# A windowed-attention, soft-MoE and ReLU-squared kernel: attention on pairs of units, scores on four quarters of the array

## The chip, the cores and the metric

The kernel runs on one NeuronCore of a Trainium2 chip. The engines are TensorE (PE, with its weight loads shown apart as PEld), VectorE (DVE), ScalarE (ACT), GpSimd (POOL) and SyncE (SP), which here only issues DMAs. The metric is the device time of one execution in microseconds; the median of the runs counts.

## The reference

Three stages follow one another. Batch is 4, there are 8 heads, 576 positions, 64 dimensions a head. The first four heads see a plain window of 32 positions, the last four a window of 32 positions four apart (dilated).

```python
scores = scale * np.matmul(q, k.transpose(0, 1, 3, 2))          # scale = 1/8
scores = np.where(masks[None], scores, -1e9)
attn = np.exp(scores - np.max(scores, axis=-1, keepdims=True))
attn = attn / (np.sum(attn, axis=-1, keepdims=True) + 1e-9)
x = np.matmul(attn, v)                       # then (4*576, 512): 2304 tokens

logits = x @ phi                             # 32 slots, 4 for each of 8 experts
d = exp(logits - logits.max(0)); d /= d.sum(0) + 1e-9       # over all tokens
slot_input = (d.T @ x).reshape(8, 4, 512)
slot_out[e] = np.maximum(slot_input[e] @ w1[e], 0.0) @ w2[e]    # 1024 inner
c = exp(logits - logits.max(1)); c /= c.sum(1) + 1e-9       # over the slots
x = c @ slot_out

r = np.maximum(x @ w_in, 0.0)                # 2048 inner
out = (r * r) @ w_out
```

w_in and w_out arrive as 64-bit floats and are converted on the chip; all else is 32-bit.

## The kernel before, in words

**Units and chunks.** A unit is one batch and one pair of heads (`kc`): 16 units in all, with keys and queries laid out as 128 rows, 64 for each of its two heads. The dilated heads are stored so that their window is contiguous too. A unit has 9 blocks of 64 queries; each block needs 96 keys. Three blocks make a chunk, so there are 48 chunks of [128 query rows (2 heads x 64), 3 blocks, 96 keys], 12 a batch.

**A chunk's way.** Each step has one letter in the written order.

- `f0`, `f1`: `fill_qz` (L310 on DVE, L312 on ACT) copies the queries of each head, times -1/8, into a block-diagonal tile `qz`; the zeros beside them were written once at the start (L262).
- `q`: `ch_qk` writes the mask into a PSUM bank with an identity matmul (L320, bf16), and adds the scores of three blocks with three matmuls of 128 rows, 128 columns of weights and 96 columns that move (L323). The block-diagonal tile keeps the two heads apart.
- `m`: the minimum of the negated scores (L337, DVE). `x`: three exps with their sums (L343, ACT).
- `n`: the sum plus 1e-9 (L350) and its reciprocal (L351) on DVE, then the normalization on POOL (L352).
- `t`: three transposes (L358). `T`: the copy `pts` from PSUM (L363, DVE or ACT). `p`: six matmuls with the values, one for each block and head (L372). `P`: the copy of the result `o` into `x` transposed (L391, one piece for plain heads; L398, two pieces with a stride for dilated heads).
- `d`: `dup_v` on POOL (L199) repeats values that two neighbouring blocks share.

**A batch's way.** `L`: the logits (L443). `Le`, `L2`, `D`, `De`, `ce`, `cn`: the softmaxes over tokens and slots, with running maxima from batch to batch. `X`: transposes of x back (L409), `Xe` their copy (L420). `S`: sums of x into slots (L428), collected in one bank for all four `kc`, and `Se` the update of the running sums (L538, L540). The last batch has a version of its own, with slot sums one `kc` at a time (`Z`, L525), and the transposed slots (`st`, L566), from which the experts start.

**Order.** All engines follow an order written out by hand: the strings `PRE`, `ATT` (repeated for three batches) and `TAILSEQ` list the steps, and a token is skipped where its condition doesn't hold yet. Each engine works through its instructions in this order. Behind attention `SEQ` orders the experts (`y`, L759; `x`, L882), the conversion of w_in and w_out (L829 to L867) and the last stage (L979 to L1013), which takes the longest.

**Memory.** Loads go through one SP queue into a ring of 22 buffers: keys and queries, then values of every unit, then 16 loads of w1, 16 of w2 (1 MB each), then w_in and w_out, for which only five of the buffers serve. A load is issued when a buffer comes free, in this order: a unit's keys and queries are freed with the scores of its last chunk, its values with the last matmul on them. PSUM has eight banks: two each for scores, transposes and values, one for logits and x transposed back (`m`), one for slot sums.

```python
nc.tensor.matmul(s, lhsT=identb, rhs=mb[:, o:o + 3, :], start=True, stop=False)        # L320
for i in range(3):
    blk = 3 * c + i
    nc.tensor.matmul(s[:, i, :], lhsT=qz[n % QZ_BUFS][:, i, :],                        # L323
                     rhs=qk_t[u][1][:, QB * blk:QB * blk + KB], start=False, stop=(i == 2))
```

## Time and profile before

| | |
|---|---|
| median of 3 runs | 400.65 us (400.21 to 400.71) |
| profiled execution | 399.67 us |
| its span, first to last instruction | 397.9 us |
| mean granted clock of TensorE | 0.991 |
| busy share of the span | PE 97%, DVE 69%, ACT 62%, POOL 21% |
| moved by DMA | 70.11 MB |

The profile is of one execution. Busy time of an engine is the time in which it had an instruction under way; PE's matmuls are pipelined, so that PE counted as busy is not PE at its peak. One fp32 matmul shows as two records where the weights are loaded twice. The chain of waits goes back from the last instruction to what released it, step by step. A DMA share is the mean busy share of the core's 16 DMA engines, and can pass 1 a little.

### The profile page before, as it was taken

The page shows a single profiled execution, that of the slowest core. Times are in us where ns is not written, and L with a number is a line of the kernel's source. Part 1 is how long each engine was busy: PE and PEld are TensorE (multiplying, and loading weights), DVE is VectorE, ACT ScalarE, POOL GpSimd, SP SyncE. Part 2 cuts the span into 40 slices and gives each one's busy share as a digit, 9 for nine tenths or more (in the row PEclk, how much of TensorE's full clock was granted, in tenths as well). Part 3 has the DMA queues.
Part 4 walks back from the last instruction along what each step waited for, and adds up shares of the span by engine and source line. Part 5 has one row for each costly group of instructions (what it writes and reads, how often), then busy time and mean ns, then how long its engine had stood idle before and what let it go on. Part 6 is the DMA issues. An engine that isn't in the chain of part 4 may idle for free.

```text
span 397.9 us, 8017 instructions
## 1 busy us (share of the span) xinstructions
PE 387.8 (97%) x2880; PEld 296.3 (74%) x2880; DVE 274.1 (69%) x630; ACT 247.9 (62%) x738; POOL 83.8 (21%) x167
## 2 busy tenths in 40 slices
PE   7999999999999999899999999999999999999996
PEld 4887887887875334678776877788888888888885
DVE  3799888888763226999999999655454555544554
ACT  5688888888954104899698876564444445644450
POOL 2787775757621001110000002000000000000000
PEclk9699999999999999999999999999999999999999
DMA  7998599989989999963356200021000000400004
GB/s 220 417 417 328 182 296 298 325 306 294 316 313 343 390 387 377 387 210 117 111 208 211 107 0 2 0 105 55 0 2 0 0 2 1 158 2 1 0 2 158
DMA packets 31991, 70.11 MB, mean 176 GB/s; under 512 B 2256, under 2 KB 5328, under 8 KB 31952
## 3 DMA queue, kind: packets, MB, share of 16 engines
q1 hardware_dynamic: 31952, 69.61, 49.7%
q8 instruction: 23, 0.38, 0.4%
q14 instruction: 16, 0.13, 0.1%
HBM read 64.88 MB, written 4.72 MB: 175 GB/s over the span
## 4 chain that ended last, share of the span: by engine, by line
PE 66%; DVE 21%; issue 4%; DMA 4%; SPq 2%; ACT 1%; POOL 0%; DVEq 0%; POOLq 0%; ACTq 0%
PE acc L1007 23%; PE acc L1013 12%; PE s L323 6%; PE o L372 5%; DVE cv L847 4%; PE psh L759 4%; PE pt L358 4%; DVE lo L1001 3%; DVE slotA L842 3%; PE ph L979 3%; PE xnp L409 3%; DMA slotA<-in_w_in_dram 2%; PE s L320 2%; PE pacc L428 2%; DVE cv L838 2%
## 5 line engine op out<-in xcount | busy, mean ns | idle before, releaser
L1007 PE MATMUL acc<-wohl,hi 128*128 128x512 f32 x580 | 152.5, 396 | 0.0
L1007 PEld LDWEIGHTS acc<-wohl,hi 128*128 128x128 f32 x580 | 107.1, 189 | 22.7 <-issue 0.8
L986 ACT ACTIVATE u<-ph 128x384 f32<-128x384 f32 x96 | 46.4, 491 | 70.9 <-PE ph L979 69.8
L1013 PE MATMUL acc<-wohl,lo 128*128 128x512 f32 x290 | 84.9, 395 | 0.3 <-DVE lo L1001 0.2
L996 DVE TENSOR_TENSOR g<-u 128x384 f32<-128x384 f32 x74 | 41.1, 557 | 55.3 <-ACT u L986 55.3
L1013 PEld LDWEIGHTS acc<-wohl,lo 128*128 128x128 f32 x290 | 54.1, 188 | 13.8 <-DVE lo L1001 1.3
L1001 DVE TENSOR_TENSOR lo<-g,hi 128x384 fp32r<-128x384 f32 x96 | 52.8, 555 | 7.9
L343 ACT ACTIVATE p<-s,ns 128x96 f32<-128x96 f32 x144 | 47.4, 343 | 7.3 <-DVE ns L337 6.8
L994 ACT ACTIVATE hi<-u 128x384 fp32r<-128x384 f32 x82 | 42.9, 526 | 2.2
L352 POOL TENSOR_TENSOR p<-p,ns 128x288 f32<-128x288 f32 x48 | 32.1, 671 | 26.9 <-DVE ns L351 13.7
L713 POOL COPY c3n<-c_all 96x96 f32<-96x96 f32 x24 | 9.0, 412 | 108.9 <-PE ph L725 84.8
L343 ACT ACTIVATION_READ_ACCUMULATOR p<-s,ns 128x1 f32 x144 | 29.7, 206 | 0.0
L337 DVE TENSOR_REDUCE ns<-s 128x3 f32<-128x288 f32 x48 | 21.7, 451 | 10.7 <-PE s L323 10.4
L358 PE MATMUL pt<-ident,p 128*96 128x128 f32 x144 | 24.9, 284 | 0.6 <-POOL p L352 0.6
L199 POOL TENSOR_TENSOR slotC<-slotC,zero 32x384 f32<-32x384 f32 (+1 forms) x27 | 19.9, 746 | 6.6 <-DMA slotC<-in_vw_dram 5.5
L323 PEld LDWEIGHTS s<-slotC,qz 128*128 128x128 f32 x126 | 18.4, 216 | 2.1 <-issue 1.9
L323 PE MATMUL s<-slotC,qz 128*128 128x96 f32 x126 | 19.1, 293 | 0.7 <-DVE qz L310 0.7
L847 DVE CUSTOM_DVE_ANT_0 cv<-slotA,cv 128x2048 uint16<-128x2048 uint16 (+1 forms) x18 | 18.8, 1044 | 0.1
L842 DVE SCALAR_TENSOR_TENSOR slotA<-slotA 128x1024 int32<-128x1024 int32 (+1 forms) x18 | 18.7, 1041 | 0.2
L358 PEld LDWEIGHTS pt<-ident,p 128*96 128x96 f32 x144 | 16.6, 136 | 2.4 <-issue 1.1
L979 PE MATMUL ph<-C3a,M 96*128 96x384 f32 x48 | 16.3, 350 | 2.0 <-DVE M L957 1.1
L835 ACT ACTIVATE slotA<-slotA 128x1024 int32<-128x1024 uint32 (+1 forms) x18 | 18.0, 1004 | 0.2 <-DMA slotA<-in_w_in_dram 0.2
(182 smaller groups left out, 559.2 us busy)
## 6 DMA issues: line engine op xcount, KB each, us to landing
slotB<-in_w_dram SPq DMA_DIRECT2D x14, 1024.0 KB, 6.6
slotC<-in_w_dram SPq DMA_DIRECT2D x12, 1024.0 KB, 7.0
slotA<-in_w_in_dram SPq DMA_DIRECT2D x6, 1024.0 KB, 5.4
slotA<-in_w_out_dram SPq DMA_DIRECT2D x6, 1024.0 KB, 5.0
slotA<-in_w_dram SPq DMA_DIRECT2D x5, 1024.0 KB, 6.8
slotC<-in_kq_dram SPq DMA_DIRECT2D x6, 576.0 KB, 7.8
slotB<-in_kq_dram SPq DMA_DIRECT2D x6, 576.0 KB, 8.2
out_dram<-e SPq DMA_DIRECT2D x12, 256.0 KB, 2.2
```

What stands on the lines that cost most here:

```text
L323: nc.tensor.matmul(s[:, i, :], lhsT=qz[n % QZ_BUFS][:, i, :], rhs=qk_t[u][1][:, QB * blk:QB * blk + KB], start=False, stop=(i == 2),)
L343: nc.scalar.activation(p[:, i, :], s[:, i, :], AF.Exp, bias=ng[:, i:i + 1], scale=-1.0, accum_out=sm[:, i:i + 1])
L352: nc.gpsimd.tensor_tensor(p, p, rs.unsqueeze(2).to_broadcast([128, 3, KB]), op=ALU.mult)
L358: nc.tensor.transpose(pt[:, i, :], p[:, i, :], ident)
L842: nc.vector.scalar_tensor_tensor(w[:, :, 1], w[:, :, 1], -2 ** 31, w[:, :, 0], op0=ALU.bitwise_and, op1=ALU.bitwise_or)
L847: E[e].tensor_tensor(box["yi"], box["yi"], box["w"][:, :, 1], op=ALU.add)
L986: nc.scalar.activation(r, u_t[k], AF.Relu)
L994: nc.scalar.activation(t, r, AF.Square)
L996: nc.vector.tensor_tensor(t, r, r, op=ALU.mult)
L1001: nc.vector.tensor_tensor(lo, g_t.pop(k), hi_t[k], op=ALU.subtract)
L1007: nc.tensor.matmul(a[:, c], lhsT=hi_t[k][:, sl], rhs=w[:, c], start=first, stop=False)
L1013: nc.tensor.matmul(a[:, c], lhsT=lo_t[k][:, sl], rhs=wo_hl[fc][0][:, c], start=False, stop=last)
```

## The change

Attention is planned anew. A unit is now worked on together with its neighbour (the order of `kc` becomes 0, 1, 2, 3, so that both units of a pair have the same kind of window).

- `q` works for a pair: the array is addressed as four parts of 64 rows by 64 columns. The row half is the head, the column half is the unit. Each part gets the mask by a quarter of the identity and then three score matmuls, directly from the loaded queries; the results of the two row halves go to two PSUM banks. There are 24 pair steps with 4 mask matmuls and 12 score matmuls each. The queries' block-diagonal copies (`f0`, `f1`, `qz`) are gone.
- A group is one of the two banks: one head, two units, again [128, 3, 96]; 48 groups. Mask and scores are no longer negated or scaled, so `m` takes a maximum, negates it, and multiplies it by 1/8 in an instruction of its own (DVE, 128x3), and the exp scales by 1/8.
- `n` is split: `r` is the sum plus 1e-9 and the reciprocal, `n.g` or `n.v` the normalization on POOL or on DVE (36 and 12 times).
- A values step `p` needs the transposed copies of both groups of a pair.
- PSUM: scores have three banks in place of two, transposes one in place of two, `m` two in place of one, and the bank of the slot sums is gone: every batch sums its slots one `kc` at a time (`slot_pe`), through `m`, and updates the running sums in four pieces.
- Copies `T` are on ACT 30 times and on DVE 18 times (23 and 25 before), copies `P` on ACT 8 times and on DVE 40 times (39 and 9 before), copies `Xe` on ACT 22 times and on DVE 10 times (28 and 8 before). There are four buffers for `pts` (two before) and three for `xn` (two before).
- The first loads: both units of the first pair in pieces, the first three blocks of each ahead. The warm-up matmuls at the start are 6 in place of 4.
- One string `ATT` holds the whole order of attention, every step once, and takes the place of `PRE`, three times `ATT`, and `TAILSEQ`. Steps of the softmaxes are cut finer (`Le` and `Lx`, `De` and `Dx`, `ce` and `cx`, `cn` and `cg`). `SEQ` is as it was.

```diff
-KCS = (0, 2, 1, 3)
+KCS = (0, 1, 2, 3)
+XN_BUFS = 3
-QZ_BUFS = 3
...
-WARM0 = 4
+WARM0 = 6
...
+ATT = """
+q m m x d x q r d n.v d r t m n.g T.a m x d t x T.v d q r d n.v p r m t n.g P.a m p x d T.v P.v d t x r T.v n.g q r
+d n.v t d m p T.a m d p x P.v t d P.v x T.v q d r n.v p d r t m P.a n.g p m x T.v d P.v t x r d q T.v n.g r p m n.g
+p m P.a t d P.v x T.v d x t r q n.v T.a r m t n.g p m x T.v p d P.v t x d r q P.v n.g T.a r m p n.g m t x P.v p T.v
...
-    aq2 = attp.enter_context(tc.tile_pool(name="aq2", side="right", bufs=2))
+    aq2 = attp.enter_context(tc.tile_pool(name="aq2", side="right", bufs=4))
+    app = attp.enter_context(tc.tile_pool(name="app", side="right", bufs=4))
-    ps_s = att.enter_context(tc.tile_pool(name="ps_s", bufs=2, space=PSUM))
-    ps_t = att.enter_context(tc.tile_pool(name="ps_t", bufs=2, space=PSUM))
+    ps_s = att.enter_context(tc.tile_pool(name="ps_s", bufs=3, space=PSUM))
+    ps_t = att.enter_context(tc.tile_pool(name="ps_t", bufs=1, space=PSUM))
-    ps_m = att.enter_context(tc.tile_pool(name="ps_m", bufs=1, space=PSUM))
+    ps_m = att.enter_context(tc.tile_pool(name="ps_m", bufs=2, space=PSUM))
...
-        if u == 0:
-            cuts = ((t, src, KW, KW + 3 * QB), (cb, cst, 0, 128 + 4 * KB), (t, src, WIN, WIN + 3 * QB),
-                    (t, src, KW + 3 * QB, KW + S), (t, src, WIN + 3 * QB, KW), (cb, cst, 128 + 4 * KB, cb.shape[1]))
-            for dst, x, lo, hi in cuts:
+        if u < 2:
+            mid = 128 + 4 * KB
+
+            def part(dst, x, lo, hi):
                 o = 0 if dst is cb else WIN
                 nc.sync.dma_start(dst[:, lo:hi], x[:, lo - o:hi - o])
+
+            part(t, src, KW, KW + 3 * QB)
+            if u == 0:
+                part(cb, cst, 0, mid)
+            part(t, src, WIN, WIN + 3 * QB)
+            rest.append((t, src, KW + 3 * QB, KW + S))
+            rest.append((t, src, WIN + 3 * QB, KW))
+            if u == 1:
+                for r in rest:
+                    part(*r)
+                part(cb, cst, mid, cb.shape[1])
...
+    units_of = [(2 * (n // 3), 2 * (n // 3) + 1, n % 3) for n in range(3 * len(units) // 2)]
+    NCH = len(units_of)
...
-    def fill_qz(n, h, e):
-        u, c = chunks[n]
-        dst = qz[n % QZ_BUFS][64 * h:64 * h + 64, :, QB * h:QB * h + QB]
-        src = qk_t[u][0][64 * h:64 * h + 64, 3 * c:3 * c + 3]
-        if e == "v":
-            nc.vector.tensor_scalar(dst, src, -SCALE, None, op0=ALU.mult)
-        else:
-            nc.scalar.mul(dst, src, -SCALE)
...
     def ch_qk(n):
-        u, c = chunks[n]
-        s = ps_s.tile([128, 3, KB], F32, tag="s", name="s")
-        o = min(c, 1) if units[u][1] < 2 else (9, 3, 6)[c]
-        nc.tensor.matmul(s, lhsT=identb, rhs=mb[:, o:o + 3, :], start=True, stop=False)
-        for i in range(3):
-            blk = 3 * c + i
-            nc.tensor.matmul(
-                s[:, i, :], lhsT=qz[n % QZ_BUFS][:, i, :], rhs=qk_t[u][1][:, QB * blk:QB * blk + KB],
-                start=False, stop=(i == 2),
-            )
-        s_t[n] = s
+        u0, u1, c = units_of[n]
+        s = [ps_s.tile([128, 3, KB], F32, tag="s", name="s") for _ in range(2)]
+        o = min(c, 1) if units[u0][1] < 2 else (9, 3, 6)[c]
+        rows = [slice(0, 64), slice(64, 128)]
+        for i in range(2):
+            for h in range(2):
+                nc.tensor.matmul(
+                    s[h][rows[i]], lhsT=identb[rows[h], rows[h]], rhs=mb[rows[h], o:o + 3, :], start=True, stop=False,
+                )
+        for j in range(3):
+            blk = 3 * c + j
+            for i, u in enumerate((u0, u1)):
+                for h in range(2):
+                    nc.tensor.matmul(
+                        s[h][rows[i], j, :], lhsT=qk_t[u][0][rows[h], blk, :],
+                        rhs=qk_t[u][1][rows[h], QB * blk:QB * blk + KB], start=False, stop=(j == 2),
+                    )
+        for h in range(2):
+            s_t[2 * n + h] = s[h]
         if c == 2:
-            free(("load_qk", u))
-
-    ng_t = {}
-
-    def ch_max(n):
+            free(("load_qk", u0))
+            free(("load_qk", u1))
+
+    def ch_max(g):
         ns = ap3.tile([128, 6], F32, tag="ns", name="ns")
-        ng = ng_t[n] = ns[:, 0:3]
-        sum_t[n] = ns[:, 3:6]
-        nc.vector.tensor_reduce(ng, s_t[n], axis=AX.X, op=ALU.min)
-
-    def ch_exp(n):
-        p = p_t[n] = ap3.tile([128, 3, KB], F32, tag="p", name="p")
-        s, ng, sm = s_t.pop(n), ng_t.pop(n), sum_t[n]
+        ng = ng_t[g] = ns[:, 0:3]
+        sum_t[g] = ns[:, 3:6]
+        nc.vector.tensor_reduce(ng, s_t[g], axis=AX.X, op=ALU.max, negate=True)
+        nc.vector.tensor_scalar(ng, ng, SCALE, None, op0=ALU.mult)
...
-                p[:, i, :], s[:, i, :], AF.Exp, bias=ng[:, i:i + 1], scale=-1.0, accum_out=sm[:, i:i + 1]
+                p[:, i, :], s[:, i, :], AF.Exp, bias=ng[:, i:i + 1], scale=SCALE, accum_out=sm[:, i:i + 1]
...
+    def ch_rec(g):
+        rs = sum_t[g]
+        nc.vector.tensor_scalar(rs, rs, 1e-9, None, op0=ALU.add)
         nc.vector.reciprocal(rs, rs)
-        nc.gpsimd.tensor_tensor(p, p, rs.unsqueeze(2).to_broadcast([128, 3, KB]), op=ALU.mult)
-
-    def ch_t(n):
+
+    def ch_norm(g, e):
+        p, rs = p_t[g], sum_t.pop(g)
+        {"v": nc.vector, "g": nc.gpsimd}[e].tensor_tensor(
+            p, p, rs.unsqueeze(2).to_broadcast([128, 3, KB]), op=ALU.mult
+        )
...
+    def ch_pv(g):
+        n, i = divmod(g, 2)
+        u, c = units_of[n][i], units_of[n][2]
         o = ps_v.tile([128, 3, QB], F32, tag="v", name="o")
-        for i in range(3):
+        for j in range(3):
             for h in range(2):
                 nc.tensor.matmul(
-                    o[64 * h:64 * h + 64, i, :],
-                    lhsT=v_t[u][:, 3 * c + i, 64 * h:64 * h + 64],
-                    rhs=t[:, i, QB * h:QB * h + QB],
+                    o[64 * h:64 * h + 64, j, :],
+                    lhsT=v_t[u][:, 3 * c + j, 64 * h:64 * h + 64],
+                    rhs=pt_t[2 * n + h][:, j, QB * i:QB * i + QB],
...
-    def slot_kc(b, kc, half):
-        if ("acc", None) not in ps_of:
-            ps_of["acc", None] = ps_m.tile([96, DM], F32, tag="acc", name="pacc")
-        t = ps_of["acc", None]
-        x = xn_t.pop((b, kc, half))
-        for j in range(3):
-            nc.tensor.matmul(
-                t[32 * j:32 * j + 32, 128 * kc:128 * kc + 128],
-                lhsT=ps_of["dn"][:, half, 32 * j:32 * j + 32],
-                rhs=x[:, j, :],
-                start=(half == 0), stop=(half == 1),
...
     def slot_pe(b, kc):
-        pool, tag = ((ps_m, "m"), (ps_m, "acc"), (ps_v, "v"), (ps_v, "v"))[kc]
-        t = ps_of["acc", kc] = pool.tile([96, 128], F32, tag=tag, name="pacc")
+        t = ps_of["acc", b, kc] = ps_m.tile([96, 128], F32, tag="m", name="pacc")
...
+    def slot_ev(b, kc):
+        t = ps_of.pop(("acc", b, kc))
+        a = acc[:, 128 * kc:128 * kc + 128]
...
-        return np.where(band & same, 0.0, BIG)
+        return np.where(band & same, 0.0, -BIG)
```

## Rows read from the trace of the kernel before

**Rows 1.** Stages; columns: us, PE, PEld, DVE, ACT, POOL busy, clock, DMA share, GB/s

```profile
0.00:40.30 40.30, 36.50 (x357) 28.99 (x360) 30.33 (x98) 29.32 (x139) 25.50 (x64) 0.92 0.92 343
40.30:67.70 27.40, 27.40 (x367) 22.64 (x370) 22.82 (x74) 23.90 (x113) 18.82 (x31) 1.00 0.82 258
67.70:95.10 27.40, 27.40 (x367) 22.63 (x370) 22.76 (x76) 23.67 (x111) 17.92 (x30) 1.00 0.92 308
95.10:115.20 20.10, 20.06 (x287) 15.77 (x289) 14.05 (x47) 14.71 (x68) 11.56 (x19) 1.00 0.94 319
...
141.60:157.50 15.90, 15.78 (x135) 5.16 (x127) 6.90 (x14) 3.34 (x8) 2.06 (x9) 1.00 1.06 382
```

**Rows 2.** Chain that ended last, 30 to 96 us: start us, us, what

```profile
30.98 1.09 ACT p L343 x6
...
76.15 0.35 PE pacc L428 x6
76.50 0.23 PE s L320
76.73 0.64 PE s L323 x6
77.37 0.33 PE pt L358 x3
...
78.03 0.50 PE o L372 x12
...
85.29 0.57 PE pacc L428 x12
...
95.09 1.43 PE psl L443 x24
```

**Rows 3.** DVE by line, 67.7 to 95.1 us; the last row is all of attention

```profile
L337 DVE TENSOR_REDUCE ns<-s 128x3 f32<-128x288 f32 x12 | 5.4, 452 | 2.9 <-PE s L323 2.9
L310 DVE TENSOR_SCALAR qz<-slotC 64x192 f32<-64x192 f32 x15 | 5.0, 343 | 0.4 <-PE s L323 0.2
L363 DVE COPY pts<-pt 96x384 f32<-96x384 f32 x6 | 3.2, 536 | 0.0
L350 DVE TENSOR_SCALAR ns<-ns 128x3 f32<-128x3 f32 x12 | 3.0, 247 | 0.4 <-ACT p L343 0.2
...
L538 DVE COPY acc<-pacc 96x512 f32<-96x512 f32 x1 | 0.7, 657 | 0.0
...
L509 DVE TENSOR_TENSOR lc<-lc,nq 96x192 f32<-96x192 f32 x1 | 0.4, 356 | 0.0
...
L391 DVE COPY xr<-o 128x192 f32<-128x192 f32 x1 | 0.3, 328 | 0.0
...
L350 DVE TENSOR_SCALAR ns<-ns 128x3 f32<-128x3 f32 x48 | 13.7, 286 | 1.7 <-ACT p L343 1.0
```

**Rows 4.** DVE and POOL in order of time, 61 to 67 us

```profile
61.83 0.67 POOL L352 TENSOR_TENSOR p<-p,ns 128x288 f32<-128x288 f32 x1 [2.16 <-DVE ns L351]
62.19 0.33 DVE L350 TENSOR_SCALAR ns<-ns 128x3 f32<-128x3 f32 x1
...
66.73 0.49 DVE L350 TENSOR_SCALAR ns<-ns 128x3 f32<-128x3 f32 x1
```

**Rows 5.** What SP's DMA queue waited for: us in total, times, longest us

```profile
SPq L208 <- PE o L372: 26.0, 8, 3.7
SPq L208 <- PE s L323: 19.3, 8, 2.7
```

**Rows 6.** The same chain behind the experts' matmuls

```profile
148.69 8.84 DMA slotA<-in_w_in_dram
```

**Rows 7.** DVE and PE in order of time, at the start

```profile
6.08 0.46 DVE L337 TENSOR_REDUCE ns<-s 128x3 f32<-128x288 f32 x1 [0.21 <-PE s L323]
...
14.60 0.91 PE L372 MATMUL o<-pts,slotC 96*64 96x64 f32 x12
```

265 lines of the change are left out of this document (109 added, 156 removed).

## The prediction

> **What bounds the kernel now.** I read the stages first, each beside the busy time of its engines; then the chain of waits inside one batch of attention; then the instructions of that batch by engine; then what the DMA queue waits for; last the chain behind attention.
>
> Attention is the stretch from 0 to 123.1 us. The logits of the first batch stand at 40.3, those of the second at 67.7, of the third at 95.1, of the last at 115.2; the reader is to see that in the two middle batches, 27.40 us each, PE is busy for 27.40, VectorE (DVE) for 22.8, ScalarE (ACT) for 23.7 to 23.9, GpSimd (POOL) for 17.9 to 18.8 [rows 1]. Before 40.3 nothing is full on average: PE's granted clock was 0.92 on average and DVE stood still for 10.0 us, most of it at the start. In the chain of a middle batch every piece is PE's [rows 2]: mask 0.23 and scores 0.64 (0.87 a chunk, 12 chunks), three transposes 0.33, values 0.50, transposes of x as long as the others (8 times), slot sums, logits 1.43. 12 x (0.87 + 0.33 + 0.50) + 8 x 0.33 + 1.43 is 24.5; slot sums and small transposes fill the rest. So here a shorter PE program is a shorter batch, down to the next engine.
>
> Behind attention the chain goes over the experts' matmuls to the first loads of w_in, which end at 157.5 [rows 6]; from 141.6 on the DMA share is 1.06 [rows 1]. The weights get buffers as attention gives them up: the queue spent 45.3 us waiting for PE's scores and values before it issued the w1 loads [rows 5].
>
> **Scores by quarters.** A pair of chunks cost PE 2 x 0.87 = 1.74. Now it is 4 masks of 288 columns and 12 matmuls of 96 columns, each on a quarter of the array. No row of before has a matmul on half the array's rows; it has them on column parts. Six records of slot sums take 0.35, twelve 0.57 [rows 2]: six more cost 0.22, so a change of shape costs 0.35 - 0.22 = 0.13. The values, 64 x 64 output parts, take (0.50 - 0.13) / 12 = 0.031 a record. A mask without its change of shape is 0.23 - 0.13 = 0.10. I take 24 records at 0.031, masks two at a time 0.20, and 0.13: 1.07. Ends: logits are 0.0596 a record of 192 columns, three side by side (1.43 / 24), so one of 96 columns alone is 0.089. Four side by side: 24 x 0.022 + 0.10 + 0.13 = 0.76. None side by side: 24 x 0.089 + 0.40 + 0.13 = 2.67, an estimate from the same rows. I stay at 1.07 because the values row is nearest: parts of 64 columns too.
>
> The Trainium skill, TensorEngine Tiling (Array Packing), Tiling Modes, says that different tiles load weights and multiply in parallel; by it the pair is 0.76. Its Performance Considerations say that tiling speeds up TensorE but not the emptying of PSUM, which speaks against the change. By the two together the batch would be DVE's and the sum below would hardly move; the trace agrees with the first for column parts (0.22 for six records) and shows nothing of row parts.
>
> PE per middle batch: 27.4 - 12 x 0.87 + 6 x 1.07 + 6 x 0.13 (scores no longer have the transposes' shape) = 24.2; slot sums go from single pieces to fours, -0.2: 24.0. With the ends 22.1 and 33.6.
>
> **DVE.** 18 of 24 query fills go, at 0.343 and overlapping their neighbours a little: 6.0. A scaling of the negated maximum comes in, 12 of the kind of L350 at 0.247, 3.0 [rows 3]. Copies pts 6 to 3: -1.6. Copies of o into x move from ACT: 2 of 12 were DVE's, 9 or 10 are; a plain one is 0.33, a scattered one two pieces, for which I take 0.58 (two plain ones are 0.66, these are shorter): +3.4. Two normalizations a batch come from POOL; before shows none on DVE, and I take 0.44, between 0.36 (192 columns) and 0.54 (a 384-column copy): +0.9. One copy of slot sums in 512 columns (0.66) becomes four at most 0.36: +0.7. One more copy of xn 0.5, the logits copy leaves, -0.3. 22.8 - 6.0 + 3.0 - 1.6 + 3.4 + 0.9 + 0.7 + 0.5 - 0.3 = 23.4. ACT gives up six fills and most copies of o and takes three or four pts: under 21. POOL gives two normalizations of 0.67: 16.7.
>
> So a batch has PE 24.0 and DVE 23.4, nearly level. Two engines in order, each waiting for the other, don't both run without a gap; PE ran gapless only with the others at 83 to 87% [rows 1]. I take DVE at 94%: 23.4 / 0.94 = 25.0, and 2.4 saved in each of the two batches.
>
> The scaling also lengthens the way from scores to exp, by 0.25. Two banks at once out of three is the added wait: the next pair's scores start when the first exp group of this pair has freed its bank; then 1.07 + 0.45 + 0.25 until ACT can go on, with the second group's exp (1.09, [rows 2]) inside. Period 1.09 + 1.77 = 2.9, against 25.0 / 6 = 4.2. Behind a waiting score on PE stand transposes and values, for which the copies wait; 1.3 of slack covers one such piece, not three. The single bank of transposes costs 0.33 + 0.54 a group, and other PE work stands between.
>
> **First batch.** DVE's work to 40.3 becomes 17 maxima 7.7, 17 scalings 4.9 (0.29, the mean of all), 16 sums and reciprocals 7.5, 5 normalizations 2.2, 9 pts 4.8, 9 copies of o 4.1: 31.2, against 30.33. Both units' first pieces must land (five issues, not three), so the first maximum stays near 6.1 [rows 7]; but it then has two groups, and more loads behind it. 6.1 + 31.2 / 0.94 = 39.3: 1.0 saved. In SP's queue the first value load moves behind three more issues, 1.3 us later; the first values matmul was at 14.60 [rows 7], and POOL's duplication, which waits for that load, lies before it with about that much room. If not, 1.3 is lost at a time when DVE has other work.
>
> **Last batch.** Two more values steps than before are left for this stretch (12 against 10, as the pairs run less far ahead), and two fewer chunks of scores: PE 20.06 - 5 x 0.87 + 3 x 1.07 + 2 x 0.50 + 0.33 + 0.4 (shapes) = 20.7; DVE: 6 maxima and scalings 4.2, 7 sums and reciprocals 3.2, 3 normalizations 1.3, 3 pts 1.6, 12 copies of o 5.5, the batch's own steps about 4, in all 20. I take 21.0, which is 0.9 more than 20.1. The 7.9 behind it (last logits, x transposed, slot sums) has the same instructions: 0. The two more warm-up matmuls lie before the first pieces of both units have landed.
>
> **Sum.** -1.0 - 2 x 2.4 + 0.9 = -4.9 for the end of attention. The weight loads keep up with batches of 25.0: a share of 0.92 becomes 0.92 x 27.4 / 25.0 = 1.01, under the 1.06 seen [rows 1]. But a pair frees its two value buffers close together at the end, one load of 1 MB more to come late; at 308 / 0.92 = 335 GB/s that is 3 us of transfer [rows 1], of which I charge 1.0. Behind that, 34.4 us to the first w_in and the rest shift whole. -3.9. The profiled execution took 399.67 (span 397.9 and 1.8 around it), the median of the runs is 400.65, 0.98 above: 399.67 - 3.9 + 0.98 = 396.7.
>
> **Rivals.** *More comes of it.* Four parts side by side (0.76) and scalings at their unblocked 0.17: DVE 22.4, 23.8 a batch, 3.6 saved twice, 2.4 in the first, 0.4 lost in the last, 1.0 to the loads: -8.2, 392.4. For it: column parts do run together. Against it: DVE's copies from PSUM have no reason to shrink.
>
> *The loads hide it.* Attention ends 4.9 earlier, w_in only 1.5: 399.1. For it: 0.92 to 1.06 of the DMA engines' time is taken from 67.7 on [rows 1]. Against it: those 45.3 us in which the queue waited for buffers.
>
> *DVE is blocked by POOL (slower).* A 128x3 scaling takes 0.33 when it starts beside POOL's normalization and ends with it [rows 4], 0.15 to 0.17 when it doesn't. 48 such scalings are added, before exp, and 12 normalizations that read two tiles of SBUF. At 0.41, between the blocked 0.33 and the 0.49 of another such pair, each of the 60 costs 0.16 more than I took: 10 us at 94%, 406.7. It decides from a mean of 0.31 on (60 x 0.06 / 0.94 = 3.9); a whole batch before had 0.247 and all 48 had 0.286, so this is near [rows 3].
> The Trainium skill, SBUF — State Buffer, Who interferes with whom, names such a lock between DVE and GpSimd, held for the whole instruction; the 0.33 agrees with it, and by it a wait can reach POOL's whole 0.67.
>
> *The parts don't run together.* PE 33.6 a batch, 6.2 more twice, about 5 in the first (nine pairs at 0.93 more, part of it beside DVE), 5.4 in the last: 23 more, 423.
>
> **Chances.** Forecast 0.42 (its own range 393.5 to 399.5), more 0.17, loads 0.12, DVE blocked 0.20, no parallel parts 0.07; 0.02 for anything else. 0.2% of this kernel is 0.8 us, about what a measurement can tell from no change: faster means under 399.85. Forecast 0.40, more 0.17, loads 0.07: 0.64 faster. The rest of the forecast and of the loads and a little of the blocked case: 0.08 the same. 0.28 slower. The range 390 to 407 leaves out the serial case, a third of the blocked one and the lower part of the good one.
>
> **What would show it.** Right: logits of batches 1 to 3 near 39, 64 and 89, attention's end near 118, pairs of scores near 1.07, DVE over 90% in the middle batches and no longer PE alone in the chain, the first w_in near 153.5. Wrong: 24 records of scores over 1.74 (no parallel parts); 128x3 scalings over 0.31 (blocked); PE waiting for exp at the scores (banks); the end of attention earlier and w_in not (loads); a granted clock under 1.00 behind 20 us, for which I have charged nothing because PE stays above 90% busy.

## The result, and the profile after

The change is slower, by 0.7%. 20 executions after it have a median of 404.07 us, 20 before it 400.70; the ratio over all executions is 1.0066 (95% interval 1.0043 to 1.0090; the medians alone give 1.0084). Forecast were 396.7 in a range of 390 to 407: the time lies in the range, but it moved the other way. The one execution of the changed kernel that was profiled first took 400.34 (span 398.6), the least of the 20. The same kernel, profiled again as the first experiment (the control below), took 405.67 (span 403.9), which is nearer to the median. Both are needed:

| | before | after, first profile | after, control |
|---|---|---|---|
| first logits start (us) | 40.22 | 41.72 | 42.93 |
| second and third batch | 27.40, 27.40 | 25.68, 24.57 | 25.67, 24.57 |
| last batch | 20.01 | 21.03 | 21.03 |
| last logits to experts | 8.03 | 10.86 | 12.43 |
| first 80 expert matmuls | 8.72 | 8.72 | 11.51 |
| span | 397.9 | 398.6 | 403.9 |

But for the last two rows, a duration and the span, each number is a start of PE's logits or expert matmuls, or a difference of two. From before to the control the stages add +2.7, -1.7, -2.8, +1.0, +4.4 and +2.8, together 6.4; the span grew by 6.0. The two middle batches gave what was forecast; the two ends of attention and the experts behind it took more back.

The stages of the first profile after, beside [rows 1] (columns as there):

```profile
0.00:41.80 41.80, 30.47 (x453) 20.30 (x456) 28.25 (x92) 20.98 (x107) 24.95 (x63) 0.84 0.85 312
41.80:67.60 25.80, 23.04 (x454) 17.54 (x457) 24.37 (x86) 21.25 (x103) 18.71 (x31) 1.00 0.62 203
67.60:92.10 24.50, 22.18 (x451) 17.30 (x448) 23.29 (x84) 20.47 (x98) 16.01 (x27) 1.00 0.99 341
92.10:113.20 21.10, 19.20 (x367) 14.82 (x361) 18.43 (x67) 14.27 (x63) 6.39 (x10) 1.00 1.02 349
```

In the middle batches the full engine is no longer PE (23.04 of 25.8, 22.18 of 24.5) but DVE (24.37 and 23.29, 94 to 95%). The clock of the first stage is 0.84 where it was 0.92, and the DMA share of the second stage is 0.62 where it was 0.82.

A piece of the chain of waits in the third batch, beside [rows 2] (start us, us, what):

```profile
85.34 0.25 PE s L330 x4
85.59 0.58 PE s L337 x24
86.16 0.45 DVE ns L351
...
87.17 0.46 DVE ns L351
...
87.65 0.34 DVE ns L352
...
88.27 0.76 DVE xr L418 x4
```

The reader is to see that a pair of scores takes 0.25 + 0.58 = 0.83, against 2 x 0.87 before, and that the chain then goes on DVE from the maximum (L351) to the scaling (L352) and the copies of o; before, every piece was PE's.

DVE by line in the third batch, and the scaling over all of attention, beside [rows 3] (count | busy us, mean ns | idle before):

```profile
L351 DVE TENSOR_REDUCE ns<-s 128x3 f32<-128x288 f32 x12 | 5.3, 446 | 0.1
...
L352 DVE TENSOR_SCALAR ns<-ns 128x3 f32<-128x3 f32 x12 | 4.2, 351 | 0.4
...
L364 DVE TENSOR_SCALAR ns<-ns 128x3 f32<-128x3 f32 x12 | 2.9, 239 | 0.0
...
L418 DVE COPY xr<-o 128x96 f32<-128x96 f32 (+2 forms) x9 | 2.3, 341 | 0.0
...
L369 DVE TENSOR_TENSOR p<-p,ns 128x288 f32<-128x288 f32 x3 | 1.7, 581 | 0.1
```

```profile
L352 DVE TENSOR_SCALAR ns<-ns 128x3 f32<-128x3 f32 x48 | 17.4, 362 | 1.6
```

The scaling took 0.351 on average in this batch and 0.362 over all 48, where 0.247 was taken; a normalization 0.581 (0.44 was taken), a piece of a scattered copy of o 0.341. The instructions of DVE in this batch add up to 27.7 us, where they added up to 25.6 before: 2.1 more, against the forecast 0.6. That DVE is nevertheless busy for only 0.5 longer (23.29, before 22.76) is because its records overlap by more (4.4 us, before 2.8). So the forecast of this batch came true with terms that did not.

The chain behind attention, beside [rows 2, 6]:

```profile
113.18 1.34 PE psl L457 x24
...
123.93 8.72 PE psh L724 x80
...
149.51 8.97 DMA slotA<-in_w_in_dram
```

The w_in load of the chain lands at 158.48, 0.95 later than before (148.69 + 8.84 = 157.53), though the middle batches had given 4.5. (The prediction calls it the first w_in; two other loads of w_in are issued ahead of it, at 113.86 and 143.97.)

The control's clock and engines in stretches of 10 and of 2 us, and its first expert matmuls in its chain:

```profile
10.00:20.00 10.00, 6.12 (x65) 4.30 (x64) 5.84 (x19) 4.45 (x25) 7.42 (x14) 0.50 0.99 376
20.00:30.00 10.00, 7.59 (x142) 5.62 (x144) 9.24 (x25) 5.20 (x28) 8.24 (x15) 0.84 1.02 417
30.00:40.00 10.00, 8.76 (x145) 6.54 (x138) 7.83 (x30) 5.21 (x28) 5.65 (x11) 0.66 0.60 245
...
118.00:120.00 2.00, 1.31 (x13) 0.80 (x14) 1.97 (x11) 1.01 (x3) 0.00 (x0) 1.00 1.06 385
120.00:122.00 2.00, 1.18 (x30) 0.94 (x33) 1.66 (x7) 0.36 (x1) 0.00 (x0) 1.00 1.05 378
122.00:124.00 2.00, 2.00 (x28) 1.36 (x20) 1.01 (x5) 0.19 (x1) 0.51 (x1) 0.52 1.05 387
...
128.00:130.00 2.00, 2.00 (x12) 0.39 (x8) 0.43 (x1) 1.24 (x2) 0.00 (x0) 0.50 0.22 54
```

```profile
126.70 11.51 PE psh L724 x80
```

PE is busy 6.1, 7.6 and 8.8 of 10 us at the start, at a granted clock of 0.50, 0.84 and 0.66 (0.50 is the lower of its two levels, 1.2 GHz). At 118 to 122 it is busy 2.5 of 4, and from 122 to about 132 it has the lower level: the last slot sums and the first expert matmuls run at it. At 128 to 130 the DMA engines are nearly idle (0.22); that the buffers which those matmuls read come free later would explain it, which no run tested. Before, PE was busy through all of this stretch, at 1.00, and in the first profile after it stayed at 1.00 too. Of the 20 executions, the eight with a mean clock of 0.977 or more have a mean of 402.0 us, the other twelve 404.5.

The Trainium skill, TensorE: Matmul & The Clock Gate, What's actually happening, says that the throttled state is the default, that activity releases it, and that the same kernel can differ from run to run in how many matmuls it catches. The trace agrees: one program, half clock at 122 to 130 in one execution and not in another. The page puts the loss by the ramp to full clock at under 1% of a typical kernel. Here the half clock comes in the middle of the kernel, and the first 80 expert matmuls alone lost 2.8 us to it, 0.7% of 404, about the size of the whole result.

### The profile page after: what moved, and what is told of

Same layout as the page of the kernel before. It is cut to its first block, busy times and chain, and to the rows that moved or that the text cites. A ratio compares the mean times of both kernels' runs of the same rounds, so it can differ in the third digit from the quotient of the medians.

```text
span 398.6 us, 8620 instructions
## 1 busy us (share of the span) xinstructions
PE 372.0 (93%) x3220; PEld 276.3 (69%) x3220; DVE 278.8 (70%) x664; ACT 232.6 (58%) x677; POOL 75.9 (19%) x154
## 4 chain that ended last, share of the span: by engine, by line
PE 49%; DVE 35%; issue 6%; DMA 3%; SPq 3%; POOL 1%; ACT 1%; DVEq 0%; POOLq 0%; ACTq 0%
PE acc L972 23%; PE acc L978 12%; DVE cv L812 4%; DVE ns L351 4%; PE psh L724 4%; DVE slotA L807 3%; DVE lo L966 3%; PE ph L944 3%; DVE ns L352 3%; DMA slotA<-in_w_in_dram 2%; DVE pts L382 2%; PE pt L377 2%; DVE cv L803 2%; DVE g L961 1%; DVE ns L364 1%
## 5 line engine op out<-in xcount | busy, mean ns | idle before, releaser
L358 ACT ACTIVATE p<-s,ns 128x96 f32<-128x96 f32 x144 | 47.2, 341 | 16.2 <-DVE ns L352 13.5
L959 ACT ACTIVATE hi<-u 128x384 fp32r<-128x384 f32 x82 | 42.9, 526 | 2.2
L377 PE MATMUL pt<-ident,p 128*96 128x128 f32 x144 | 26.5, 296 | 12.4 <-DVE pts L382 5.8
L369 POOL TENSOR_TENSOR p<-p,ns 128x288 f32<-128x288 f32 x36 | 24.1, 669 | 31.1 <-DVE ns L365 20.6
L377 PEld LDWEIGHTS pt<-ident,p 128*96 128x96 f32 x144 | 15.0, 132 | 17.2 <-POOL p L369 4.2
L351 DVE TENSOR_REDUCE ns<-s 128x3 f32<-128x288 f32 x48 | 21.3, 444 | 3.9 <-PE s L337 3.6
L217 POOL TENSOR_TENSOR slotC<-slotC,zero 32x384 f32<-32x384 f32 (+1 forms) x24 | 18.1, 763 | 6.2 <-DMA slotC<-in_vw_dram 5.5
L352 DVE TENSOR_SCALAR ns<-ns 128x3 f32<-128x3 f32 x48 | 17.4, 362 | 1.6
L382 ACT COPY pts<-pt 96x384 f32<-96x384 f32 x30 | 14.3, 476 | 6.5 <-PE pt L377 6.1
```

The source lines that it names most:

```text
L351: nc.vector.tensor_reduce(ng, s_t[g], axis=AX.X, op=ALU.max, negate=True)
L352: nc.vector.tensor_scalar(ng, ng, SCALE, None, op0=ALU.mult)
L358: nc.scalar.activation(p[:, i, :], s[:, i, :], AF.Exp, bias=ng[:, i:i + 1], scale=SCALE, accum_out=sm[:, i:i + 1])
L377: nc.tensor.transpose(pt[:, i, :], p[:, i, :], ident)
L959: nc.scalar.activation(t, r, AF.Square)
```

## Experiments

All are the changed kernel with the edit named. Times are medians; 404.07 is the change, 404.64 the control. "Experts" is the start of the first expert matmul. The runs fall into four groups, e1 to e4, e5 to e8, e9 to e11 and e12; the kernel before, run beside each, had medians of 400.12, 401.12, 400.56 and 400.72, so that medians of different groups compare to about 1 us, and the ratios compare better. The starts are those of one profiled execution each. Four profiles have the first batch of the change as it was (the first, e1, e3, e6), and their first logits come at 41.7 to 43.5; e7 and e9 share one first batch too, and have 39.5 and 41.3. A difference of less than 2 us in that column is no finding.

| label | median us | ratio to before (95%) | first, last logits | experts | span |
|---|---|---|---|---|---|
| e1_control | 404.64 | 1.0097 (1.0060-1.0134) | 42.9, 114.2 | 126.6 | 403.9 |
| e2_scale_act | 399.21 | 0.9979 (0.9955-1.0004) | 39.8, 109.1 | 121.5 | 398.8 |
| e3_tail | 402.44 | 1.0034 (1.0010-1.0058) | 42.9, 114.2 | 123.6 | 399.3 |
| e4_fill | 406.35 | 1.0130 (1.0088-1.0173) | 46.1, 116.8 | 128.6 | 404.9 |
| e5_act_tail | 397.78 | 0.9919 (0.9902-0.9935) | 39.4, 108.8 | 118.1 | 395.3 |
| e6_tail_fill | 402.51 | 1.0039 (1.0025-1.0054) | 43.5, 114.4 | 125.9 | 400.6 |
| e7_norm_v | 401.19 | 1.0000 (0.9977-1.0023) | 39.5, 110.5 | 122.9 | 400.2 |
| e8_act_tail_norm | 396.30 | 0.9887 (0.9869-0.9904) | 38.5, 107.9 | 117.2 | 393.9 |
| e9_tail_norm | 399.25 | 0.9971 (0.9951-0.9991) | 41.3, 112.0 | 121.4 | 398.0 |
| e10_norm_first | 402.17 | 1.0042 (1.0024-1.0059) | 40.1, 111.7 | 124.1 | 401.4 |
| e11_act_tail_first | 396.12 | 0.9885 (0.9858-0.9912) | 39.6, 109.0 | 118.4 | 395.0 |
| e12_light_fill | 396.21 | 0.9883 (0.9855-0.9910) | 36.3, 106.8 | 116.1 | 391.9 |

**e1_control.** No edit.

> The changed kernel, unchanged, timed again and profiled a second time. Its median over 20 runs was 404.07 us, 3.4 above the median before, while the one execution that was profiled took 400.34. Theory 1 (the granted clock): a second profiled execution that is 2 to 4 us longer shows more half-clock stretches ahead of 115 us than the first did (there 13 to 23 and 34 to 37 us), and the last logits later than 113.2 us. Theory 2 (the loads): the same clock as in the first, and the extra time behind 124 us, where the first w_in load lands later than 158.5 us. Time by both: 402 to 405 us.

Neither theory holds as it was put. The last logits came 1.2 us later than in the first profile, after a first batch with more half clock; but e3, with the clock of the first profile there (0.66, 0.83, 0.83), has its first logits at 42.94, as the control, so the clock does not explain the 1.2. The larger part (1.6 up to the experts and 2.8 in their first 80 matmuls, of 5.3 in the span) lies behind the last logits, in the half clock at 122 to 132. Theory 2 is out, since the clock there was not the same: the w_in load that is issued at 149.51 in the first profile is issued 4.5 later, behind 80 expert matmuls that end 5.6 later.

**e2_scale_act.**

```diff
-        nc.vector.tensor_scalar(ng, ng, SCALE, None, op0=ALU.mult)   # in ch_max
+        nc.scalar.mul(ng, ng, SCALE)                                 # in ch_exp, before the exponentials
```

> The 48 scalings of the negated maximum move from DVE to ACT, ahead of the three exponentials. They took 48 x 0.362 = 17.4 us of DVE, which was busy 9.4 to 9.6 of every 10 us from 20 to 110 us; on ACT they should take about 0.2 each (nearest row: the 128x32 copy of slotT, 0.19), 9.6 us, on an engine that was busy 5 to 9 of 10. Theory A (DVE held up by POOL is what the change pays for): each batch of 12 scalings gets 3 to 4 us shorter until PE bounds at about 24, the last logits come at 106 to 109 instead of 113.2 us, and the time falls by 3 to 7 us, to 397 to 401. Theory B (the chain of one unit's maximum, scaling, exponential bounds, or ACT becomes the bound): the logits stay within 1 us and the time within 402 to 405. Theory C (the loads): the logits come earlier but the first w_in load still lands at 158 to 159 us, and the time stays within 1.5 us of 404.

5.4 us less (4.9 against the median of 20), within theory A's range, but not where A had it. Against the control the first batch is 3.1 shorter (1.9 against the first profile), the middle ones go from 25.67 to 24.56 and from 24.57 to 24.41, and the last is 0.7 shorter; the tail is as long as the control's (12.43) and at half clock too. DVE by line and the engines in the third batch:

```profile
L364 DVE TENSOR_SCALAR ns<-ns 128x3 f32<-128x3 f32 x13 | 4.7, 360 | 1.0 <-ACT p L358 1.0
...
L356 ACT ACTIVATE ns<-ns 128x3 f32<-128x3 f32 x13 | 2.7, 211 | 0.4 <-DVE ns L351 0.4
```

```profile
64.40:88.80 24.40, 22.35 (x457) 17.38 (x451) 21.88 (x72) 22.00 (x111) 16.21 (x27) 1.00 0.99 333
```

DVE lost 4.2 us of scalings there and got about 1.5 back: the short instruction behind the exponentials (L364) now takes 0.360 on average, where it took 0.239. It went from 95% busy to 90% (21.88 of 24.4), and the batch hardly moved, with PE at 92% and ACT at 90%. So in the third batch the three engines are level, and the scaling was hidden; in the first batch, where they wait for one another in turn, it was on the path. Theory B holds in the third batch, A in the first; the second lies between.

How much of the scaling is waiting can be read from the first profile of the change. Nine of the 48 scalings had no POOL instruction beside them and took 0.169 each; the other 39 took 0.407 on average, up to 0.83, and most of them ended 0.02 to 0.03 behind the POOL instruction beside them. At 0.169 the 48 would have taken 8.1 us of DVE, not 17.4.

The Trainium skill, SBUF — State Buffer, Who interferes with whom, says that GpSimd and a DVE instruction in a two-port mode contend for a shared port pair, that whichever issues first has it for its whole instruction, and that the other waits. A wait that goes over to the next short instruction when its victim is removed agrees with that: 0.239 to 0.360 on a line that was not touched.

One row of this run bears on the first batch, PE's second transposes behind POOL's normalization:

```profile
14.31 0.87 PE L377 MATMUL pt<-ident,p 128*96 128x128 f32 x3 [4.51 <-POOL p L369]
```

They wait for 4.51 us, and yet the first logits come at 39.8. This wait is taken up again at e10.

**e3_tail.** Behind the last logits, the banks of four kinds of PE's results, the order, and the engine of one copy (the last `ste`, from ACT to DVE):

```diff
-        t = ps_m.tile([96, 4, 96], F32, tag="m", name="pld")
+        pool = {"dl": "m", "d": "v", "l": "t"}[parts]
+        t = ps_x[pool].tile([96, 4, 96], F32, tag=pool, name="pld")
...
-        pst = last["st", kc] = ps_t.tile([128, NS], F32, tag="t", name="pst")
+        pst = last["st", kc] = ps_s.tile([128, NS], F32, tag="s", name="pst")
...
-        tot = last["tot"] = ps_v.tile([96, 1], F32, tag="v", name="tot")
+        tot = last["tot"] = ps_s.tile([96, 1], F32, tag="s", name="tot")
...
-... Lx X.m Xe.v Xe.a X.t X.v L2.v ff X.s Xe.a Xe.v D3 Xe.a fs Xe.v Dl Xe.a fsp De3 w1 S w2 Dle ce Se S cx S cn st Se cg Se ste.a S st Se ste.a st ste.a st ste.a
+... Lx X.m Xe.v Xe.a D3 X.t X.v L2.v ff X.s Xe.a Xe.v De3 Xe.a fs Xe.v Dl Xe.a fsp S w1 S Se w2 S Se st S Se st Se ste.a st ste.a st ste.a Dle ce ste.v cx cn cg
```

> Only the stretch behind the last logits is changed: the transposes of the exponentials, those of the logits, the total and the slot transposes each get a bank that is free by then, and the last batch's slot sums stand ahead of its second softmax in the order. From the last logits to the first expert matmul took 10.75 us, 7.93 before. Theory D (the shared banks and the order there cost the 2.8): that stretch falls to 8 to 8.7 us, the experts start 2 to 2.8 us earlier, and the time falls by as much, to 401.3 to 402. Theory C (the loads): the experts start earlier, but wait for their weights, the first w_in load still lands at 158 to 159 us, and the time stays within 0.7 us of 404.

Where the 2.8 went is seen in the order of time of the first profile after (start us, us, engine, line; in brackets the idle time and what ended it):

```profile
116.81 0.34 DVE L486 COPY lsb<-psl 96x192 f32<-96x192 f32 x1
...
117.21 0.37 PE L500 MATMUL pld<-ident,dT 96*96 96x96 f32 x2
...
119.69 0.35 DVE L523 TENSOR_TENSOR lc<-pld,nq 96x192 f32<-96x192 f32 x1
...
120.19 0.42 PE L544 MATMUL pacc<-xn,dn 96*32 96x128 f32 x6 [0.82 <-DVE lc L523]
...
122.84 0.41 PE L572 MATMUL pst<-gw,acc 96*128 96x32 f32 x2 [0.28 <-ACT slotT L575]
```

The transposes of the exponentials (L500) start as soon as the copy of the logits (L486) ends, since both use one of two banks; the slot sums of the second `kc` wait 0.82 for the second softmax (L523), which reads another; each slot transpose waits for the copy of the one before it, since there is one bank for them. With the new tail this stretch takes 9.35, where it took 12.43 in the control and 10.86 in the first profile, and PE is busier:

```profile
120.00:122.00 2.00, 1.98 (x47) 1.47 (x38) 1.41 (x6) 0.19 (x1) 0.00 (x0) 1.00 1.05 383
122.00:124.00 2.00, 1.61 (x19) 1.00 (x14) 1.37 (x5) 0.73 (x3) 0.00 (x0) 1.00 1.05 388
```

```profile
123.58 8.79 PE psh L725 x80
...
142.34 14.11 DMA slotC<-in_w_dram
```

Against the control the experts start 3.0 us earlier and run at full clock in this execution (their first 80 matmuls 2.7 shorter), and the time falls by 2.2 (1.6 against the median of 20). Of the 3.0, 1.6 is the control's half clock; at full clock in both, the new tail is worth 1.5 (10.86 to 9.35). That is theory D's direction and about half of its size: it had 8 to 8.7 for the stretch and 401.3 to 402 for the time. Banks, order and the one copy were changed together and are not told apart. C holds in part: the chain now goes through a load that lands at 156.45, the last of w2, for which PE waits, and of the 5.7 us in these two stages the span shows 4.6.

The 1.3 us by which this tail is still longer than before lie at least in part on DVE. The copy of the transposed exponentials (`dn`) starts 3.93 behind the last logits before:

```profile
118.96 0.35 DVE L495 COPY dn<-pld 96x192 f32<-96x192 f32 x1
```

In this run it starts at 118.91, which is 4.68 behind them, after DVE's copies xr, lsb and xn; before, DVE had one copy of x there, and the copy lsb was ACT's. No run moved these copies.

**e4_fill.** 41 matmuls of zeros behind the steps of the first batch.

```diff
+    def fill(k):
...
+        for _ in range(k):
+            nc.tensor.matmul(
+                wt[0], lhsT=zero[:, 4:8], rhs=zero[:, 8:9].to_broadcast([128, 192]), start=True, stop=True
+            )
```

> In the first batch, matmuls of zeros (4 rows by 192 columns) are added on PE: 8 behind the second pair of scores and one behind each later group of scores, transposes and values, up to the first logits. Nothing reads them. PE was busy 6.0, 7.8 and 8.1 of 10 us at 10 to 40 us, and its granted clock was 0.65, 0.84 and 0.83 there. Theory 1 (the granted clock follows what PE does, and half clock lengthens the first batch): the clock stands at 0.95 to 1.00 from about 16 us on, the first logits come 1 to 2 us earlier than 41.8, and the time falls by 1 to 4 us, to 400 to 403. Rival (DVE bounds there, PE has slack at half clock): the clock rises, but the logits stay within 0.5 us of 41.8 and the time within 0.7 us of 404, or up to 1 us above it through the matmuls added.

```profile
10.00:20.00 10.00, 9.76 (x90) 4.51 (x89) 5.24 (x16) 3.64 (x20) 7.04 (x14) 0.86 1.00 390
```

The clock rises (0.86 where the control had 0.50), and the first logits come 3.2 us later: PE is full with zeros. This shows that zeros raise the clock, not what the clock is worth.

**e5_act_tail.** Both edits of e2 and e3.

> The scaling on ACT and the new tail together. With the scaling on ACT the last logits came at 109.1 us, but PE was granted half clock at 118 to 126 us and the first 80 expert matmuls took 11.51 instead of 8.72 us; with the new tail alone the clock stayed at 1.00 there and they took 8.79. Theory 1 (the holes in the tail cost the clock, and the clock costs the experts): the experts start at 117.5 to 118.5 us, their first 80 matmuls take 8.7 to 8.9, and the time falls to 394 to 397 us, 2 to 5 below the scaling alone. Theory C (the weight loads are a floor: with the new tail alone the chain of waits ran through a load that landed at 156.45 us, in the first profile of the changed kernel through one that landed at 158.48): the experts start as early, wait for a load that lands at 155 to 157 us, and the time stays at 397.5 to 399.

1.4 below e2, and above theory 1's range: the clock fell at 118 to 122 nonetheless, the first 80 expert matmuls took 10.49, and the span's chain goes through the w_in load:

```profile
146.25 8.94 DMA slotA<-in_w_in_dram
```

It lands at 155.19. These are theory C's numbers, but the loads are no floor. This is not the load of e3's chain, which was w2's; the same two loads are issued 3.95 (w_in, 150.20 there) and 4.85 (w2, 142.34 to 137.49) earlier than in e3, behind experts that start 5.45 earlier. So the loads move with attention.

**e6_tail_fill.** Eight matmuls of zeros in the tail, nothing else. (The expectation says ten; the order has eight `w`, and the trace 16 records, two for each. `w1` and `w2` are steps that were there before.)

```diff
-fs Xe.v Dl Xe.a fsp De3 w1 S w2 Dle ce Se S cx S cn st Se cg Se ste.a S st Se ste.a st ste.a st ste.a
+fs Xe.v w Dl Xe.a w fsp De3 w w w1 S w w w2 Dle ce Se S cx S cn st Se cg Se ste.a S st Se ste.a w st ste.a w st ste.a
```

> The changed kernel with ten matmuls of zeros (4 rows by 192 columns) on PE between the last transposes and the last slot transposes; nothing reads them, and nothing else is changed. In the second profile of the changed kernel PE was busy 1.31 and 1.18 of 2 us at 118 to 122, its granted clock was 0.50 from 122 to 131, and the time was 4 us above that of the first profile, where it stayed at 1.00. Theory 1 (the clock that falls in the tail is what the median has above the first profile): the clock stays at 1.00 there, the first 80 expert matmuls take 8.7 to 9, the experts start 1 to 2 us earlier than at 126.6, and the median falls by 2.5 to 4.5 us, to 399.5 to 401.5. Rival (the matmuls of zeros delay the real ones as in the first batch, or the clock is of no matter there): the time stays within 1 us of 404 or goes up by up to 1.5.

```profile
118.00:120.00 2.00, 2.00 (x15) 0.93 (x12) 2.00 (x9) 1.24 (x4) 0.00 (x0) 1.00 1.07 388
...
122.00:124.00 2.00, 2.00 (x40) 1.50 (x38) 1.35 (x6) 0.55 (x2) 0.51 (x1) 1.00 1.05 388
```

The clock stays at 1.00, the first 80 expert matmuls take 8.72 instead of 11.51, and the experts start 0.8 earlier though eight matmuls were added and the first logits were 0.5 later. The span is 3.3 less than the control's. The median fell by 2.1 (1.6 against the 20), between the two theories' numbers; that an execution which keeps the clock anyway has nothing to gain would explain it. All six executions have a mean clock of 0.973 to 0.978, the control's six 0.962 to 0.970. This shows the clock by itself, since no other instruction and no other bank was changed.

**e7_norm_v.** The second normalization on DVE.

```diff
-q m m x d x q r d n.v d r t m n.g T.a m x d t ...
+q m m x d x q r d n.v d r t m n.v T.a m x d t ...
```

> One word of the order: the second group's normalization is made on DVE instead of POOL. POOL began it at 13.38 us, behind two copies of value rows (11.91, 1.39 us, which waited 1.05 for a load), while its sums were ready at 10.2 and DVE was idle from 11.3 to 15.0; PE's next transposes waited 3.24 us for it, and the granted clock went to 0.50 in that stretch. Theory 3 (POOL's place in the order at the start makes the first batch late): these transposes start at 10.8 to 11.2 instead of 14.1 us, the first logits come 1 to 3 us earlier than 42.9, and the time falls by 1 to 3, to 401 to 403. Rival (the first batch is late by the loads or by DVE's work behind 20 us, and waits again at the next value load): the transposes come earlier, but the logits stay within 0.5 us of 42 to 43 and the time within 0.7 of 404.

The transposes start at 11.39 and the first logits 3.5 us earlier than the control's; the time is 2.9 below the median of 20. Theory 3 holds in its way, with transposes 0.2 later and logits 0.5 earlier than it had them, though the first 80 expert matmuls were again at half clock (11.55).

**e8_act_tail_norm.** e2, e3 and e7 together.

> All three: the scaling on ACT, the new tail, and the second normalization on DVE. If the parts add up: 1 to 2.5 us below the scaling and the tail together, 392.5 to 396. If the weight loads are a floor, no less than 397 whatever the attention gains.

396.30, 1.5 below e5 and 1.1% below the kernel before, 0.3 above the range for parts that add up. Added to e5 the third part gives 1.5 of the 2.9 that it gave alone; from 404.07 the three alone gave 4.9, 1.6 and 2.9, together 9.4, where all three give 7.8. So they add up in part. The loads are no floor at 397, though the chain again goes through the last load of w2, which lands at 151.07.

**e9_tail_norm.** e3 and e7; the scaling stays on DVE.

> The new tail and the second normalization on DVE, with the scaling left on DVE as in the change. Alone they gave 402.44 and 401.19 us (404.6 for the change in the first call). If they add up, 398.5 to 399.5: the change would then be faster than before with nothing mended but the order at its two ends and four banks, and the scaling on DVE would cost the 2 to 3 us that lie between this and all three together (396.3). If the clock in the tail also depends on what comes ahead of it (half clock for the experts with the normalization alone, 11.55 us for their first 80 matmuls), the experts' first 80 take 8.7 to 8.9 here, and the time is nearer to 398. If the scaling's blocks are what the change pays for (17.1 us of DVE), 400 to 401.5.

399.25, in the range for parts that add up: with only the two ends of attention mended, the change is 0.3% faster than before. Against e8 the scaling on DVE costs 3.0 us of the median. Of the 4.1 us between these two profiles' spans 2.9 lie in the first batch, but e7 has the first batch of this run and its first logits at 39.5, so that up to 1.9 of the 2.9 is the spread between executions. The clock still fell in the tail (first 80 matmuls 10.37).

**e10_norm_first.** One instruction moved on POOL's queue.

```diff
-q m m x d x q r d n.v d r t m n.g T.a m x d t ...
+q m m x d x q r n.v r t m n.g d d T.a m x d t ...
```

> The changed kernel with one instruction moved on one queue: POOL makes the second normalization ahead of the two copies of value rows that it waited behind (they wait for a load until 11.91 us; the sums are ready at 10.2). Every other queue is as it was. Theory 3 (it was the place on POOL's queue): PE's second transposes start at 10.9 to 11.5 instead of 14.1 us, as when DVE made it (first logits then at 39.47), the first logits come at 39.3 to 40.5, and the time is 400.5 to 402. Rival (DVE's shorter duration, or that POOL had one less to do, gave the gain there): the logits stay at 41.5 to 43 and the time at 403 to 405.

POOL and PE at the start, first of the control, then of this kernel (start us, us, engine, line):

```profile
11.91 1.39 POOL L217 TENSOR_TENSOR slotC<-slotC,zero 32x256 f32<-32x256 f32 x2 [1.05 <-DMA slotC<-in_vw_dram]
...
13.38 0.67 POOL L369 TENSOR_TENSOR p<-p,ns 128x288 f32<-128x288 f32 x1
...
14.10 0.88 PE L377 MATMUL pt<-ident,p 128*96 128x128 f32 x3 [3.24 <-POOL p L369]
```

```profile
10.34 0.67 POOL L369 TENSOR_TENSOR p<-p,ns 128x288 f32<-128x288 f32 x1
...
11.06 0.87 PE L377 MATMUL pt<-ident,p 128*96 128x128 f32 x3 [1.57 <-POOL p L369]
...
11.53 3.17 POOL L217 TENSOR_TENSOR slotC<-slotC,zero 32x256 f32<-32x256 f32 x4 [0.39 <-DMA slotC<-in_vw_dram]
```

The normalization began at 13.38 behind copies that waited for a load; ahead of them it begins at 10.34, and the copies start when their load is there, as before. PE's transposes start at 11.06, the first logits come 2.8 earlier (1.6 against the first profile), and the time is 402.17, 0.17 beyond theory 3's range (1.9 below the median of 20; by the ratios 1.0 to 2.2); most of e7's gain is the place on the queue. But this wait is not by itself what makes the first batch late: in e2 PE waited for 4.51 us at the same place, and the first logits came at 39.8. Either mend alone brings the first logits to 39.4 to 40.1 (41.3 in e9); this one together with the scaling on ACT has 39.6 (e11), e7's together with it 38.5 (e8). The tail of this run fell to half clock (first 80 matmuls 11.56).

**e11_act_tail_first.** e2, e3 and e10.

> The scaling on ACT, the new tail, and the second normalization on POOL ahead of the copies. By theory 3 as fast as with that normalization on DVE (396.3), or up to 0.5 less, since DVE has 0.5 us less to do there: 395.5 to 396.5. If the normalization on DVE counted for itself, 397 to 398 as without either.

396.12, as e8 (396.30) within the noise, and 1.15% below the kernel before.

**e12_light_fill.** e11 with nine matmuls of zeros at the start.

> The fastest version so far (scaling on ACT, new tail, second normalization ahead of the copies: 396.12 us) with nine matmuls of zeros (4 rows by 192 columns) on PE at the start, where PE waits anyway: two behind the second pair of scores, four and three behind the first two groups of transposes. Nothing reads them. The profile of that version has a granted clock of 0.55, 0.79 and 0.70 at 10 to 40 us and its first logits at 39.6. Theory 1 (the half clock of the first 40 us costs time): the clock is 0.9 or more at 10 to 40, the first logits come at 37.8 to 38.8, the time at 394.5 to 395.5. Rival (the first batch waits for loads and DVE, and PE has time at half clock; 40 such matmuls made the change slower, 406.35): the clock rises, but the logits stay at 39 to 40 and the time within 0.5 us of 396.1, or up to 1 us above it.

```profile
10.00:20.00 10.00, 8.06 (x132) 5.21 (x133) 7.19 (x20) 6.12 (x32) 9.28 (x17) 1.00 0.98 386
20.00:30.00 10.00, 8.62 (x158) 6.32 (x154) 8.68 (x28) 8.06 (x46) 9.01 (x16) 0.83 1.02 418
30.00:40.00 10.00, 9.54 (x186) 6.85 (x188) 7.71 (x31) 8.62 (x47) 7.25 (x14) 1.00 0.99 380
```

The profiled execution has the clock up (1.00, 0.83, 1.00), its first logits at 36.3 and 393.69 us; but the median of seven is 396.21, and an execution with a mean clock of 1.000 took 396.93. The profile goes with theory 1, the median with the rival. What half clock in the first 40 us costs stays open.

## Why the prediction was wrong

**Scores by quarters: right, the size between the value taken and its lower end.** 0.83 a pair (0.25 for the masks, 0.58 for 24 records), where 1.07 was taken and 0.76 was the lower end. The rival without parallel parts is out.

**Middle batches: right.** Forecast 25.0 each at DVE 94%; measured 25.68 and 24.57 at 94 to 95%, 4.55 saved instead of 4.8. The 94% held; DVE's terms did not (2.1 more for 0.6), and the overlap of its records made up for them, which was luck. The Trainium skill's sentence that tiling speeds up TensorE and not the emptying of PSUM (TensorEngine Tiling (Array Packing), Performance Considerations) was weighed there, and the trace agrees as far as DVE empties PSUM: the maximum over a bank of scores takes 0.446, and took 0.452 before [rows 3]. PE went from 27.4 to 23.0 and 22.2 us a batch, the batch only to DVE's 23.3 / 0.95 = 24.5.

**Last batch: right.** +1.0 against +0.9.

**First batch: wrong, -1.0 forecast, +1.5 to +2.7 measured.** The term that failed is 31.2 / 0.94, a DVE that from 6.1 us on never waits for long: in the first profile DVE was busy for 28.25 of the 41.8 us, less than the forecast 31.2, and stood still for the other 13.5. The step behind it that failed is the cover of the later value load: POOL's duplication was to have "about that much room". The duplication had it; the normalization queued behind it on POOL had not, and PE waited 3.24 us for that (e10: 2.8 of it back by one move). The forecast named what the load delays and priced it at 1.3 at most, but not what stands behind the delayed instruction on its queue. Mended, the first logits come at 39.5 and 40.1 in e7 and e10; the forecast was 39.3. This wait is not the whole cause, since e2 keeps it (4.51 us) and has 39.8 with the scaling off DVE. As far as single profiles show, either mend alone takes back most of what both do, so the loss belongs to the wait and to DVE's longer way from scores to exp together.

**The tail: wrong, 0 forecast, +2.8 (at full clock) to +4.4 measured.** "Has the same instructions: 0" counted instructions, and neither banks nor order. The change gave a third bank to scores and took the separate bank of the slot sums; the tail's three waits are at banks that are shared by that. e3 gives 1.5 of the 2.8 back at full clock, and 3.1 of the 4.4 against the control, half clock included; the other 1.3 stand at least in part on DVE's queue, untested.

**The clock: wrong.** Nothing was charged "because PE stays above 90% busy". The trace of before spoke against that reason already: at 10 to 20 us PE was busy for 9.39 of 10 us at a granted clock of 0.67. After the change PE was busy for 30.5 of the first 41.8 us, where it had been for 36.5 of 40.3 [rows 1], and in the tail for 2.5 of 4; in the control half clock over the first expert matmuls followed (+2.8, undone by e6). Whether it comes is a matter of the execution: of the six profiles with the tail of the change as it was, five have these 80 matmuls at 10.52 to 11.56 (e1, e2, e4, e7, e10) and one at 8.72 (the first). Of the six with e3's tail, all 9.34 to 9.35 us long, two have them at 10.49 and 10.37 (e5, e9), and in four the clock stayed at 1.00 (e3, e8, e11, e12).

**The loads: about as charged.** 1.0 was charged. In the change itself no gain was left to show it: behind experts that start 0.8 later the w_in load lands 0.95 later. Where attention is mended the loads follow it with a lag: against e3 the experts start 6.4, 5.2 and 7.5 us earlier in e8, e11 and e12, and the w_in load is issued 5.4, 4.2 and 7.3 earlier, 0.2 to 1.0 less. The rival in which the loads hide the gain wanted 3.4 of 4.9 lost, and is out as well.

**DVE blocked by POOL, the slower rival (0.20): its sign was right, its place and its size were not.** The scaling's mean was 0.362, beyond the 0.31 from which that rival was to decide, and yet the middle batches came as forecast. The scaling costs 3.0 (e9 to e8) to 5.4 us (e2), more in the first batch than elsewhere by the profiles at hand. Of DVE's 17.4 us of scalings 8.1 are the scaling itself and 9.3 the wait beside POOL; how the 3.0 to 5.4 divide was not separated.

**Sum.** The middle and last batches gave -4.6 + 1.0, as forecast; +1.5 to 2.7 at the start, +2.8 to 4.4 in the tail and up to +2.8 in the experts turned that round.

## What to carry to other kernels

Where an edit makes the fullest engine's work shorter, look at the stages where that engine already waited. In this kernel the edit gained nothing there, and an instruction that stood behind a load on a side queue, a short one that a neighbour held up, or a bank now shared decided. Count banks and queue places of the stretch behind the change as strictly as its instructions. If PE gets holes, allow for its half clock over what follows them, and judge by several executions: one profile of the same program was 5.3 us of span better than the next.
